# A fused attention and expert kernel: first chunk in two halves, fewer idle products ahead of it, one transfer per expert, one more chunk loaded in both layouts, and a new order table

## The chip, the cores and the metric

The kernel runs on one core of one Trainium2 chip. The metric is the time of one execution on the device, in microseconds (us). Its engines are PE (matrix products, with weight loads shown as PEld), DVE and ACT (which both read PE's results out of PSUM), POOL, and SP, whose queue issues nearly all transfers between HBM and the core's memory.

## The reference

Attention through 32 inducing points, then a mixture of 16 experts, all in float32:

```
B, N, m, C = 4, 10048, 32, 128          # x: (4, 10048, 128), inducing: (32, 128)
def mab(q, kv):                          # softmax attention, kv is key and value
    a = softmax(q @ kv.T / sqrt(C));  return a @ kv
h   = mab(inducing, x)                   # (4, 32, 128): every point looks at all 10048 rows
att = mab(x, h)                          # (4, 10048, 128): every row looks at 32 points
# 4 groups of 4 experts; g = argmax(att @ w_group), e = argmax(att @ w_expert[g])
out = softmax weights of g and e * (relu(att @ w1[g, e]) @ w2[g, e])     # w1 128x1024, w2 1024x128
```

Each row of `att` is a mixture of the 32 rows of `h`. The kernel first takes the case that all rows of a batch pick one expert, applies the expert to the 32 points (one matrix G of 32 rows for each batch) and lets each row mix G. It counts rows for which this does not hold (`n_bad`), and a general branch, not entered here, would redo the work.

## The kernel before, in words

**Tiles.** Each of the 4 batches is cut into 5 chunks (b, k) of 4 x 512 rows (the last of 4 x 480). A chunk comes in transposed from HBM (`xk`, from `xT` or `xL`, 1 MB, C on the partitions). The first attention also needs it untransposed (`xn`). For the chunks in `LOADED` a second transfer brings that layout (`xm`, 1.03 MB); for the others PE turns the chunk (`turn`, four groups of four 128x128 transposes, L139) and ACT or DVE copies each group out (`tev`, in the helper L534).

**First attention** (`att1`, once a chunk): scores `s1` (L152), a running maximum on DVE (`mx`, L156 to L160), exponential on ACT (`ex`, L163), transpose `tr` (L173) with its copy `pev`, product with `xn` (`hq`, L186), accumulation on DVE. **After five chunks** (`mean`, `routes`): `rp`, `ap`, `same`, `hp` (L200 to L230), the routing product `R` (L240, L241), the choice of the expert on DVE (`pick`), then on SP a load of the chosen index (L281) and two transfers, w1 and w2 (L282, L283), into the two halves of one buffer. From these come z (L288), G4 (L306) and G (L312). **Second attention** (`att2`, in groups of two, two and one chunks): scores `s2` (L329), maximum and exponential (L333, L337), logits `L` (L344), gate weights. **Outputs** (`outputs`): 32 products (L383) into four PSUM banks, each emptied in one of three ways: ACT copies it (L398) and POOL scales it by the gate weight (L403); or ACT scales it in four pieces (L396); or DVE scales it (L392). Then SP stores the chunk, 1 MB (L407). 

**What sets the order.** `plan_all` numbers all operations. A table, `ORDER`, lists the numbers in the order of emission, with a letter that chooses the engine; every engine runs its own part of this list strictly in order, SP's transfers included. Buffers are taken from rings (19 large ones, `big`, for chunks, weights and outputs; 8 PSUM banks, `ps`) in the order in which the list frees them. A transfer whose buffer is still in use holds all transfers behind it on SP. Transfers also pass through eight completion semaphores in turn, so that about eight are under way at most.

**Idle products.** `IDLE` names operations ahead of which PE multiplies ones by ones into the bank that the operation is about to take (L489). A size of n stands for n//4 products 512 wide and n%4 products 128 wide. 19 units stand ahead of the first turn of chunk (0, 0); the other eight entries, 29 units, stand after the last R.

## Time and profile before

| | |
|---|---|
| median of 3 runs | 152.69 us (152.15 to 153.06) |
| the profiled execution: its time, its span | 153.44 us, 151.7 us |
| moved by transfers | 56.90 MB, read 35.50 MB, written 20.97 MB |
| busy: PE, DVE, ACT, POOL | 138.2, 112.9, 105.5, 51.1 us |

The span is the stretch that the trace covers. The page cuts it into 40 slices of 3.8 us with a busy share in tenths for each engine; further views give windows of one's choice, the instructions in order of time, the issues of transfers with their time to landing, and the chain of work that ended last. PE counts as busy in nearly all of the span, idle products and stretched waiting products included, so that a full row of PE alone tells little.

### The profile page before, as it was taken

How to read it: one execution, taken by the hardware profiler on the slowest of the kernel's cores; microseconds unless marked ns; L12 is line 12 of the kernel's file. 1: busy time of each engine (PE TensorE's matmuls, PEld its weight loads, DVE VectorE, ACT ScalarE, POOL GpSimd, SP SyncE). 2: the span in 40 equal slices, each digit the busy share in tenths (PEclk: the TensorE clock that was granted, in tenths of full speed). 3: DMA queues.
4: the chain of work that ended last, by engine and by line, in shares of the span. 5: the costliest groups of instructions: out<-in, count | busy, mean ns of one | idle time of the engine just before them, and what ended most of it. 6: DMA issues, size and time to landing. Idle time of an engine off the chain costs nothing.

```text
span 151.7 us, 5598 instructions
## 1 busy us (share of the span) xinstructions
PE 138.2 (91%) x2233; PEld 94.9 (63%) x2233; DVE 112.9 (74%) x383; ACT 105.5 (70%) x265; POOL 51.1 (34%) x70
## 2 busy tenths in 40 slices
PE   6999999999999999999999999999999999999000
PEld 3377588687636777867466786676784666775000
DVE  3056493576689898888998987998989999999500
ACT  3006375477704967788995999989999998999300
POOL 4000000000000000015394702464889998855200
PEclk9999999999999999999999999999999999999955
DMA  4999999999999999999898999979699999999980
GB/s 119 422 426 434 412 425 421 412 431 408 418 404 400 428 417 420 423 418 414 282 337 283 389 411 375 399 294 413 259 406 277 315 417 432 417 417 432 419 352 30
DMA packets 8529, 56.90 MB, mean 375 GB/s; under 512 B 1072, under 2 KB 1072, under 8 KB 2608
## 3 DMA queue, kind: packets, MB, share of 16 engines
q1 hardware_dynamic: 8352, 56.45, 93.1%
q8 instruction: 19, 0.31, 0.8%
q14 instruction: 14, 0.11, 0.2%
q10 hardware_dynamic: 144, 0.03, 0.1%
HBM read 35.50 MB, written 20.97 MB: 372 GB/s over the span
## 4 chain that ended last, share of the span: by engine, by line
PE 67%; DVE 14%; ACT 10%; issue 2%; DVEq 0%; ACTq 0%
PE ps L139 12%; PE ps L152 11%; PE ps L186 9%; PE ps L329 8%; PE ps L383 8%; PE ps L489 5%; PE ps L173 5%; ACT big L398 4%; ACT big L396 3%; PE ps L344 2%; DVE big L392 2%; ACT et L337 1%; DVE mxe L333 1%; PE ps L230 1%; PE ps L306 1%
## 5 line engine op out<-in xcount | busy, mean ns | idle before, releaser
L403 POOL TENSOR_TENSOR big<-big,gate_w 128x512 f32<-128x512 f32 x48 | 48.9, 1050 | 42.8 <-ACT big L398 33.4
L163 ACT ACTIVATE pe<-ps,nb 128x512 f32<-128x512 f32 (+1 forms) x20 | 13.7, 687 | 21.6 <-DVE nb L158 9.9
L398 ACT COPY big<-ps 128x512 f32<-128x512 f32 x48 | 26.7, 625 | 1.7 <-PE ps L383 1.0
L396 ACT ACTIVATE big<-ps,gate_w 128x128 f32<-128x128 f32 x84 | 24.3, 413 | 1.6 <-DVE n_bad L454 1.5
L383 PE MATMUL ps<-G,et 32*128 32x128 f32 x640 | 25.0, 285 | 0.0
L383 PEld LDWEIGHTS ps<-G,et 32*128 32x128 f32 x640 | 21.0, 186 | 5.5 <-ACT big L398 1.9
L139 PE MATMUL ps<-spread,big 128*128 128x128 f32 (+1 forms) x160 | 21.4, 276 | 0.1
L186 PEld LDWEIGHTS ps<-big,pt 128*32 128x32 f32 (+1 forms) x640 | 17.8, 110 | 5.9 <-issue 4.2
L186 PE MATMUL ps<-big,pt 128*32 128x129 f32 (+1 forms) x640 | 21.0, 273 | 0.0
L329 PE MATMUL ps<-big,hT 128*32 128x512 f32 (+2 forms) x192 | 20.5, 525 | 0.0
L152 PE MATMUL ps<-big,small_sb 128*32 128x512 f32 (+1 forms) x160 | 19.9, 588 | 0.0
L139 PEld LDWEIGHTS ps<-spread,big 128*128 128x128 f32 (+1 forms) x160 | 17.8, 141 | 2.9 <-issue 1.0
L156 DVE TENSOR_REDUCE mx<-ps 128x1 f32<-128x512 f32 (+1 forms) x20 | 13.5, 673 | 4.8 <-PE ps L152 4.1
L489 PE MATMUL ps<-ones 128*128 128x128 f32 (+1 forms) x48 | 15.5, 461 | 1.6 <-DVE ones L852 1.5
L129 POOL MEMSET big<- 128x16 f32 x10 | 0.8, 128 | 47.9 <-PE ps L186 44.7
L534 ACT COPY big<-ps 128x512 f32<-128x512 f32 (+1 forms) x28 | 15.6, 592 | 0.8 <-PE ps L139 0.7
L337 ACT ACTIVATE et<-ps,nce 128x512 f32<-128x512 f32 x20 | 13.8, 721 | 2.4 <-DVE nce L334 2.1
L534 DVE COPY big<-ps 128x512 f32<-128x512 f32 x12 | 8.0, 686 | 9.8 <-PE ps L139 9.7
L333 DVE TENSOR_REDUCE mxe<-ps 128x1 f32<-128x512 f32 x20 | 13.3, 667 | 0.7 <-ACT big L398 0.4
L534 ACT COPY pt<-ps 128x512 f32<-128x512 f32 (+2 forms) x20 | 10.0, 523 | 3.5 <-PE ps L173 2.8
L489 PEld LDWEIGHTS ps<-ones 128*128 128x128 f32 x48 | 8.1, 214 | 7.0 <-issue 4.7
L173 PE MATMUL ps<-spread,pe 128*128 128x128 f32 x80 | 12.2, 276 | 0.0
(118 smaller groups left out, 164.6 us busy)
## 6 DMA issues: line engine op xcount, KB each, us to landing
out<-big SPq DMA_DIRECT2D x20, 1024.0 KB, 7.7
big<-xT SPq DMA_DIRECT2D x16, 1024.0 KB, 13.4
big<-xm SPq DMA_DIRECT2D x10, 1032.0 KB, 10.1
big<-w SPq DMA_DIRECT2D x8, 512.0 KB, 6.1
big<-xL SPq DMA_DIRECT2D x4, 960.0 KB, 13.9
small_sb<-small ACTq DMA_DIRECT2D x1, 26.0 KB, 5.9
```

The lines of the kernel that those rows point to most:

```text
L139: em.nc.tensor.transpose(p[:tw, j * P:(j + 1) * P], em.t(xk[b, k])[:, j, off + t * P:off + t * P + tw], em.ident)
L152: em.nc.tensor.matmul(em.t(ps)[32 * j:32 * j + 32, :w], lhsT=em.indT, rhs=em.t(xk[b, k])[:, j, off:], start=True, stop=True)
L173: em.nc.tensor.transpose(p[:tw, t * P:(t + 1) * P], em.t(pe)[:, t * P:t * P + tw], em.ident)
L186: em.nc.tensor.matmul(h[32 * j:32 * j + 32, 0:CS], lhsT=q[:tw, t, 32 * j:32 * j + 32], rhs=x[:tw, t * J + j, :], start=(t == 0), stop=(t = ...
L329: em.nc.tensor.matmul(em.t(ps)[32 * j:32 * j + 32, c0:c1], lhsT=em.hT[b][:, P + 1:P + 1 + M], rhs=em.t(xk[b, k])[:, j, x0:x0 + c1 - c0], s ...
L337: em.nc.scalar.activation(out=em.t(et), in_=em.t(ps), func=AF.Exp, bias=em.s(nc_), scale=1.0)
L383: em.nc.tensor.matmul(em.t(pb[j])[:, t * C:(t + 1) * C], lhsT=em.t(et)[32 * j:32 * j + 32, t * P:(t + 1) * P], rhs=em.Gs[b][32 * j:32 * j ...
L396: em.nc.scalar.activation(out=q[:, t], in_=p[:, t], func=AF.Copy, scale=em.t(gt)["w"][:, r:r + 1])
L398: em.nc.scalar.copy(out=q, in_=p)
L403: em.nc.gpsimd.tensor_tensor(out=q, in0=q, in1=weights(j), op=ALU.mult)
L489: em.nc.tensor.matmul(em.t(ps)[:, 0:w], lhsT=em.ones[:, 0:P], rhs=em.ones[:, 0:w], start=True, stop=True)
L534: (self.nc.scalar.copy if engine == ACT else self.nc.vector.tensor_copy)(out=out, in_=in_)
```

## The change

- The transfer of chunk (0, 0) is cut into two of 0.5 MB (j = 0, 1 and j = 2, 3), with chunk (1, 0) issued between them. Its four turns now each take two column blocks of two j, so that two of them need only the first half; its `s1` is cut in two likewise (`s1j`).
- Ahead of the first turn stand 8 units of idle products, not 19, and 2 more before the first `s1j`. The row of ones is 128 wide and is broadcast to 512 for the wide ones. After the last R stand 37 units, not 29.
- w1 and w2 of an expert lie side by side in a new input, `w12`, and come in one transfer of 1 MB.
- `LOADED` has eleven chunks, not ten: batches 0 and 1 as before; of batches 2 and 3 now (2,0), (2,2), (2,4), (3,0), (3,1), (3,3), (3,4), where it was (2,1), (2,3), (2,4), (3,1), (3,3), (3,4). One chunk less is turned: 36 groups, not 40.
- `ORDER` is a new list of 713 operations (715 before).

```diff
-LOADED = {(0, 2), (0, 4), (1, 1), (1, 3), (2, 1), (2, 3), (2, 4), (3, 1), (3, 3), (3, 4)}
-IDLE = ((2, 19), (455, 3), (465, 2), (515, 3), (625, 4), (635, 2), (657, 4), (667, 5), (704, 6))
+LOADED = {(0, 2), (0, 4), (1, 1), (1, 3), (2, 0), (2, 2), (2, 4), (3, 0), (3, 1), (3, 3), (3, 4)}
+IDLE = ((3, 8), (182, 2), (457, 4), (467, 2), (489, 3), (517, 7), (605, 2), (619, 3), (629, 5), (651, 2), (674, 1), (679, 2), (698, 6))
...
+    def halves(b, k):
+        return [(0, J // 2), (J // 2, J)] if (b, k) == (0, 0) else [(0, J)]
...
-        def fn(e):
-            em.nc.sync.dma_start(out=em.t(xk[b, k]), in_=em.xL[b] if short else em.xT[b, k])
-        xk_at[b, k] = [op("xk", SP, fn, [], [xk[b, k]], size=512 * J * (KL if short else KW))]
+        got = []
+        for j0, j1 in halves(b, k):
+            def fn(e, j0=j0, j1=j1):
+                em.nc.sync.dma_start(out=em.t(xk[b, k])[:, j0:j1], in_=(em.xL[b] if short else em.xT[b, k])[:, j0:j1])
+            got.append(op("xk", SP, fn, [], [] if got else [xk[b, k]], soft=got[-1:], size=512 * (j1 - j0) * (KL if short else KW)))
+        xk_at[b, k] = got
...
-        for t in range(TK):
+        if (b, k) == (0, 0):
+            banks = [(t, t + 2, j, j + 2) for j in (0, 2) for t in (0, 2)]
+        else:
+            banks = [(t, t + 1, 0, J) for t in range(TK)]
...
-            em.nc.sync.dma_start(out=em.t(w12)[:, 0:F], in_=em.w1[bass.ds(i, 1)].rearrange("o d f -> d (o f)"))
-            em.nc.sync.dma_start(out=w2(), in_=em.w2[bass.ds(i, 1)].rearrange("o (p n) d -> p (o n) d", n=FB))
+            em.nc.sync.dma_start(out=em.t(w12), in_=em.w12[bass.ds(i, 1)].rearrange("o p f -> p (o f)"))
...
 ORDER = """
-1a 0a 206a 706a 2a 6a 3b 4a 5b 7b 8a 357a 17a 10a 45a 27a 11a 19a 12a 23a 28a 35a 178a 25a 205a 18a 20a 9a 47a 21a 53a 13a 63a 46a 29a 51a 234a 49a
...
+181a 700a 0a 3a 48a 180a 1a 701a 11a 19a 2a 37a 5a 182a 184a 186a 47a 6a 208a 236a 9a 185b 190a 12a 183a 65a 4b 188a 21a 187a 27a 191a 192a 193a 13a
```

What the new table does is seen at three places. In the rows below, a number behind `ps_` or `big_` is a buffer's; `x4` counts instructions; L numbers of the new kernel are some 10 to 13 higher than the old ones for the same operation.

PE at its start, before. L489 are idle products, L139 turns, L152 `s1`; `big_92` is chunk (0, 0), `big_95` chunk (0, 1).

```order
L489 MATMUL ps_122<-ones 128x512 x4
L489 MATMUL ps_122<-ones 128x128 x3
L139 MATMUL ps_122<-spread,big_92 128x128 x4
L139 MATMUL ps_123<-spread,big_92 128x128 x4
L139 MATMUL ps_124<-spread,big_92 128x128 x4
L139 MATMUL ps_125<-spread,big_92 128x128 x4
L152 MATMUL ps_126<-big_92,small_sb 32x512 x4
L152 MATMUL ps_127<-big_95,small_sb 32x512 x4
```

And after. L501 are idle products, L149 turns, L165 `s1`; `big_92` is again chunk (0, 0), `big_94` is chunk (1, 0).

```order
L501 MATMUL ps_122<-ones 128x512 x2
L149 MATMUL ps_122<-spread,big_92 128x128 x4
L501 MATMUL ps_123<-ones 128x128 x2
L165 MATMUL ps_124<-big_92,small_sb 32x512 x2
L149 MATMUL ps_125<-spread,big_92 128x128 x4
L149 MATMUL ps_123<-spread,big_94 128x128 x4
L149 MATMUL ps_126<-spread,big_94 128x128 x4
L149 MATMUL ps_127<-spread,big_94 128x128 x4
L149 MATMUL ps_128<-spread,big_92 128x128 x4
L165 MATMUL ps_129<-big_94,small_sb 32x512 x4
L165 MATMUL ps_124<-big_92,small_sb 32x512 x2
```

PE now begins on a half chunk; chunk (1, 0) fills the time until the second half of (0, 0).

SP at its start, before: all loads of `xT` or `xL`; after the first come (0, 1), (0, 3), (0, 2), (1, 0), (1, 2) and (0, 4).

```order
L116 DMA big_92<-xT 128x2048
L116 DMA big_95<-xT 128x2048
L116 DMA big_96<-xT 128x2048
L116 DMA big_97<-xT 128x2048
L116 DMA big_98<-xT 128x2048
L116 DMA big_99<-xT 128x2048
L116 DMA big_101<-xL 128x1920
```

And after: half of (0, 0), (1, 0), the other half, (0, 1), (0, 2), (0, 3), (0, 4).

```order
L121 DMA big_92<-xT 128x1024
L121 DMA big_94<-xT 128x2048
L121 DMA big_92<-xT 128x1024
L121 DMA big_95<-xT 128x2048
L121 DMA big_97<-xT 128x2048
L121 DMA big_98<-xT 128x2048
L121 DMA big_101<-xL 128x1920
```

Only one chunk of batch 1 now stands ahead of the end of batch 0, where two stood.

SP from the third expert's weights to the last expert's, before. L121 is a load of an untransposed chunk, L407 a store, L281 the read of the chosen index.

```order
L282 DMA big_105<-w 128x1024
L283 ISA
L283 DMA big_105<-w 128x1024
L121 DMA big_109<-xm 128x2064
L407 DMA out<-big_108 128x2048
L407 DMA out<-big_98 128x2048
L407 DMA out<-big_97 128x2048
L407 DMA out<-big_91 128x2048
L407 DMA out<-big_93 128x2048
L281 TENSOR_LOAD pi_1821
```

And after, where L419 is a store and L294 the read of the index:

```order
L295 DMA big_101<-w 128x2048
L419 DMA out<-big_99 128x2048
L419 DMA out<-big_98 128x2048
L419 DMA out<-big_100 128x2048
L419 DMA out<-big_107 128x2048
L419 DMA out<-big_102 128x2048
L294 TENSOR_LOAD pi_1832
```

The last load of a chunk now stands ahead of the third expert's weights. In both lists four stores stand ahead of the third expert's weights, five between them and the last expert's, and eleven behind those.

## The prediction

> **What bounds the kernel now.** I read the page first, then the start in order of time, the transfers' landings, a table of windows, and the chain of waits.

> ```profile
> span 151.7 us, 5598 instructions
> DVE  3056493576689898888998987998989999999500
> ACT  3006375477704967788995999989999998999300
> DMA  4999999999999999999898999979699999999980
> PE 67%; DVE 14%; ACT 10%; issue 2%; DVEq 0%; ACTq 0%
> ```

> ACT and DVE are half empty in the first third and full in the last, while the transfer engines are full nearly throughout. The windows tell the stages apart (columns: PE, PEld, DVE, ACT, POOL busy with instruction counts, clock, transfer share, GB/s):

> ```profile
> 3.00:6.50 3.50, 3.50 (x5) 1.35 (x4) 0.00 (x0) 0.00 (x0) 0.00 (x0) 1.00 1.00 410
> 8.60:60.00 51.40, 51.15 (x756) 36.43 (x758) 37.38 (x109) 30.04 (x63) 0.26 (x2) 1.00 1.01 418
> 60.00:95.00 35.00, 35.00 (x645) 24.26 (x635) 30.43 (x115) 29.57 (x74) 13.37 (x14) 1.00 0.97 371
> 95.00:121.00 26.00, 25.81 (x514) 17.67 (x505) 23.63 (x87) 24.94 (x69) 19.55 (x20) 1.00 0.90 337
> 121.00:143.00 22.00, 19.09 (x329) 13.16 (x329) 20.06 (x69) 19.50 (x59) 16.07 (x16) 1.00 1.01 423
> ```

> Against the 423 GB/s of the last stage, the queue loses (423-371) x 35 + (423-337) x 26 = 4.06 MB of carrying between 60 and 121 us, worth 9.6 us. Before 60 and after 121 it loses next to nothing. ACT has 5.4 us idle from 60 to 95 and 1.1 us from 95 to 121. The end itself is the queue's:

> ```profile
> 113.46 1.06 SPq L283 DMA_DIRECT2D big<-w  x1
> big<-w SPq DMA_DIRECT2D x1, 512.0 KB, 7.1
> 114.62 28.60 SPq L407 DMA_DIRECT2D out<-big  x11
> 142.89 0.33 SPq L407 DMA_DIRECT2D out<-big  x1
> out<-big SPq DMA_DIRECT2D x1, 1024.0 KB, 7.6
> ```

> The last expert's weights land at 113.46 + 7.1 = 120.6. Behind them go eleven stores, 11 x 1.049 MB / 423 GB/s = 27.3 us, so the last could land at 147.9; it lands at 142.89 + 7.6 = 150.5, 1.2 us ahead of the end. So the time is when the last expert's weights are through the queue, plus about 30 us. These weights wait for the last R, and what leads there is PE until 96 us and then ACT, as the chain of waits has it (start, length, what):

> ```profile
> 94.35 0.88 PE ps L186 x32
> 95.23 1.10 PE ps L383 x29
> 96.39 0.59 ACT big L398
> ...
> 105.91 0.41 ACT hs L217
> ```

> **The start.** Rows in order of time, with the landings:

> ```profile
> 0.75 0.39 SPq L116 DMA_DIRECT2D big<-xT  x1
> big<-xT SPq DMA_DIRECT2D x1, 1024.0 KB, 5.8
> 1.46 7.29 PE L489 MATMUL ps<-ones 128*128 128x512 f32 x14 [1.46 <-DVE ones L852]
> 5.89 0.34 PEld L489 LDWEIGHTS ps<-ones 128*128 128x128 f32 x1 [0.52 <-issue]
> 6.75 0.34 PEld L489 LDWEIGHTS ps<-ones 128*128 128x128 f32 x1 [0.52 <-issue]
> 7.49 0.19 PEld L489 LDWEIGHTS ps<-ones 128*128 128x128 f32 x1 [0.41 <-issue]
> 7.92 0.64 PEld L489 LDWEIGHTS ps<-ones 128*128 128x128 f32 x5 [0.24 <-issue]
> 8.59 1.91 PE L139 MATMUL ps<-spread,big 128*128 128x128 f32 x16
> 10.43 1.92 PE L152 MATMUL ps<-big,small_sb 128*32 128x512 f32 x16
> ```

> Chunk (0, 0) has landed at 0.75 + 5.8 = 6.55, and PE multiplies ones until 8.59: 2.04 us given away. The first half, 0.524 MB less at 410 GB/s, should land 1.28 us earlier, at 5.3. The new idle products, two wide ones of two passes at 0.86 us (5.89 to 6.75), run from about 1.2 to 4.6, so PE waits some 0.7 us, then works. But PE cannot keep all of it, since the queue delivers at its own pace:

> ```profile
> 4.19 0.44 SPq L116 DMA_DIRECT2D big<-xL  x1
> big<-xL SPq DMA_DIRECT2D x1, 960.0 KB, 18.2
> 9.01 0.33 SPq L116 DMA_DIRECT2D big<-xT  x1
> big<-xT SPq DMA_DIRECT2D x1, 1024.0 KB, 20.8
> 26.02 0.96 PE L152 MATMUL ps<-big,small_sb 128*32 128x464 f32 x8
> 32.38 1.09 PE L139 MATMUL ps<-spread,big 128*128 128x128 f32 x8
> ```

> The chunk issued at 4.19 lands at 22.4 and is first used at 26.02; the one issued at 9.01 lands at 29.8 and is used at 32.38. So a load lies 2.6 to 3.6 us before its use, and 2.0 us at the first. PE can run ahead by 2 to 2.6 us until it meets the queue. Bounds: -2.3 us, and +0.3 where the clock (below) takes it back. I take -1.7, nearer the full gain, since work runs in a stretch in which PE had none.

> **The turn that goes.** Sixteen transposes took 8.59 to 10.43, so four groups cost 1.84 us, which PE no longer spends. PE is on the path until 96 us, so all of it counts: -1.84 (bound 0, where ACT holds the same place). Its four evictions lie beside PE and count as nothing; were that cover gone, they would be worth 4 x 0.59 = 2.4 us of ACT:

> ```profile
> L534 ACT COPY big<-ps 128x512 f32<-128x512 f32 x27 | 15.1, 592 | 0.8 <-PE ps L139 0.7
> L534 DVE COPY big<-ps 128x512 f32<-128x512 f32 x12 | 8.0, 686 | 9.8 <-PE ps L139 9.7
> L398 ACT COPY big<-ps 128x512 f32<-128x512 f32 x48 | 26.7, 625 | 1.7 <-PE ps L383 1.0 <-issue 0.7
> L396 ACT ACTIVATE big<-ps,gate_w 128x128 f32<-128x128 f32 x84 | 24.3, 413 | 1.6 <-DVE n_bad L454 1.5
> L489 PE MATMUL ps<-ones 128*128 128x128 f32 x32 | 5.0, 283 | 0.1
> ```

> **What the table does to ACT.** Over the whole list ACT copies 52 banks instead of 48 (26.7 / 48 = 0.556 us each) and scales 19 in four pieces instead of 21 (4 x 24.3 / 84 = 1.16 us each), with two more `tev`: +2.2 - 2.3 + 1.1 = +1.0 us. DVE loses two scalings and six `tev` at about 8.0 / 12 = 0.67 us: -5 us. Behind the third expert's load the list holds 30 copies in both, but 12 four-piece scalings instead of 14: 2.3 us of ACT work moved forward, out of the stage that ACT fills and into the one where it has 5.4 us idle. This is what lets the earlier PE through to the last R; by itself I count it 0 (bounds -2.3 and +1.0). POOL's 4 more scalings end nothing.

> **The loads and the queue.** One more `xm`, 1.057 MB / 423 GB/s = 2.5 us. It is issued ahead of the third expert's weights, where the queue loses 9.6 us anyway, and that is its cover; without it, it costs all 2.5. It can still make a store behind it late, so of 0 to 2.5 I take +1.0. On SP, (1, 0) is moved ahead of the second half of (0, 0); this delays the end of that chunk to about 5.3 + 2.5 + 1.3 = 9.1, while PE holds one turn of (0, 0) and three of (1, 0) for that time. One transfer fewer for each expert saves SP one issue (1.06 us in the row of L283), but the bytes are the same and the queue behind is never empty there, so I take 0 (bound -1.1). It also spares a semaphore of the eight, which the halves use once.

> **Idle products in the tail.** 8 units more, at most 0.31 us each (5.0 / 32 a record, two records a unit): 2.5 us on a PE whose other work is then below its time. I take 0; the bound is +1, if they hold a bank that another product wants.

> **Sum.** -1.7 - 1.84 + 1.0 = -2.5 us. The profiled execution took 153.44 us (span 151.7 and 1.7 around it) and would take 150.9; the median of the runs lies 0.75 lower, so I say 152.69 - 2.5 = 150.2 us. The eleven stores at the end are as before.

> **Rivals.**
> *The clock stays low.* Up to 6.75 the passes stand 0.86 us apart, then 0.74, then 0.43: PE ran at half pace until about 7.4, 5.9 us after its first product. If it needs 5.9 unbroken us, and the new start breaks at 4.6, full pace comes at 5.3 + 5.9 = 11.2, by which PE has done 2.95 us of work; before it had done 2.6. The gain is then 0.3 and the time 151.6. If the waits for (1, 0) near 7.8 break it again, full pace comes at 13.7 with some 3.9 us done against 5.1: 1.2 us behind, 153.0. I take 152.3. Against it: the order holds idle products and `s1j` in the gap. [...]

> ```profile
> 21.53 2.35 PE L139 MATMUL ps<-spread,big 128*128 128x128 f32 x20
> ```

> After the start PE does nothing but transposes for over 2 us and their pace (0.11 us each) does not fall, though that shows a clock kept, not one gained.

> *The queue is the bound (slower).* If the 9.6 us of gaps come from buffers and from SP's strict order, not from late outputs, the earlier PE fills none of them, and the load adds 2.5 us: 155.2. It decides once the gaps shrink by less than 2.5 us. For it: the transfers are at 418 to 423 GB/s outside those stages. Against it: the eleven stores took 2.6 us more than the queue needs, so outputs are late, and those move with PE and ACT.

> *ACT sets the end and nothing changes.* ACT has 1.0 us more work and was busy 24.94 of 26 us from 95 to 121. If it cannot start earlier, PE's 3.5 us end as waiting: 152.7.

> *More is gained.* If the load hides wholly and the start gives its 2.3: -4.1, and a little from ACT's forward 2.3, 148.2.

> **How the numbers follow.** Chances: forecast 0.52 (149.0 to 151.5), clock 0.15, queue 0.12, ACT 0.13, more 0.08. The range 148.2 to 152.9 leaves out the queue case and about a third of the clock's. A change of 0.5% (0.76 us) is about what can be told from none. Faster: 0.51 of the forecast, all of "more", a third of the clock's and 0.02 of ACT's, 0.66. Slower: the queue and a third of the clock's, 0.17. Same: the rest, 0.17, most of it ACT's.

> **What would show it.** Right: the first turn at about 5.3; the pace of products doubling by 7.5 to 8; the first R about 2 us earlier; the last expert's weights landing near 118 with the queue at 380 GB/s or more from 60 to 121; eleven stores behind them as before. Wrong: half pace beyond 11 us, chunk loads landing after PE is ready for them, or 371 and 337 GB/s again in the middle.

## The result, and the profile after

| | before | after |
|---|---|---|
| first comparison, 4 runs each | 152.42 us (151.93 to 153.06) | 154.3 us (153.87 to 154.92) |
| second comparison, 23 and 12 runs | 152.91 us (152.00 to 153.39) | 154.73 us (151.45 to 157.58) |
| profiled execution of the first comparison: time, span | 153.44, 151.7 us | 154.92, 153.1 us |

The forecast was 150.2 us, 2.5 us less than before; the first comparison shows 1.88 us more. The ratio of the first comparison is 1.0107 with an interval of 1.0063 to 1.0150. The second gives 0.9970 (0.9928 to 1.0012), but such a ratio leaves out every run more than 1.5% above the fastest of its kernel, and here the scatter itself is the result; so from here on the text goes by medians of all runs, less the median of the kernel before in the same comparison: +1.88 and +1.82 us. The scatter is the kernel's own, since three kernels of the table below (e7, e13, e19) scatter by 0.5 us or less.

The page of the kernel after: its span, three rows of 40 slices, and the chain by engine.

```profile
span 153.1 us, 5560 instructions
DVE  3006285264799997889959988988889988999700
ACT  3024847835646778994989979857879889899500
DMA  3999999999999999999899999999999999999970
PE 75%; DMA 9%; DVE 7%; issue 2%; ACT 1%; SPq 0%; DVEq 0%; ACTq 0%
```

The chain has moved from ACT (10%, now 1%) to PE and to transfers (9%). The same windows as before say where:

```profile
8.60:60.00 51.40, 51.35 (x729) 35.31 (x726) 33.15 (x105) 32.59 (x71) 0.25 (x2) 1.00 1.01 420
60.00:95.00 35.00, 35.00 (x673) 25.63 (x677) 29.74 (x110) 30.24 (x79) 14.54 (x15) 1.00 0.98 383
95.00:121.00 26.00, 24.86 (x461) 15.83 (x457) 22.65 (x83) 20.63 (x53) 21.09 (x21) 1.00 0.98 364
121.00:143.00 22.00, 20.90 (x377) 15.19 (x369) 19.67 (x67) 19.90 (x58) 16.76 (x17) 1.00 0.99 411
```

From 95 to 121 us ACT is busy 20.63 us, not 24.94: the relief came. By the prediction's own measure the queue now loses (423-383) x 35 + (423-364) x 26 = 2.93 MB, worth 6.9 us in place of 9.6. The gaps shrank by 2.7 us, about the 2.5 us that the added load needs, and no more: from 60 to 121 us the queue carried 1.1 MB more than before, and the load has 1.06 MB. But PE, which hardly idled from 95 to 121 us before (busy 25.81 of 26), now idles 1.1 us there. The view of waits names what it waits for, of before and then of after (total, times, longest):

```profile
PE ps L489 <- DVE ones L852: 1.5, 1, 1.5
PE ps L451 <- DVE t L447: 0.5, 1, 0.5
```

```profile
PE ps L395 <- issue: 1.3, 3, 0.9
PE ps L501 <- DVE ones L864: 1.1, 1, 1.1
PE ps L149 <- DMA big<-xT: 1.0, 1, 1.0
PE ps L300 <- DMA big<-w: 0.8, 1, 0.8
```

The new waits are of three kinds: one at the start for the first half chunk (L149), one for the last expert's weights (L300), and three, 1.3 us together, with no releaser at all ("issue") in the middle of the output products L395. Two of these last three and the one for the weights lie on the chain of waits:

```profile
99.24 0.25 issue
...
105.14 0.89 issue
...
113.81 8.82 DMA big<-w
```

The start in order of time (PE alone):

```profile
1.06 3.78 PE L501 MATMUL ps<-ones 128*128 128x512 f32 x4 [1.06 <-DVE ones L864]
...
5.81 1.09 PE L149 MATMUL ps<-spread,big 128*128 128x128 f32 x4 [0.97 <-DMA big<-xT]
...
7.68 1.92 PE L165 MATMUL ps<-big,small_sb 128*32 128x512 f32 x4
```

The first turn begins at 5.81 instead of 8.59, but PE is at half pace until 9.68 us (7.37 before), and half a `s1` (L165) takes 1.92 us, as long as two whole ones did in the row of before (10.43). R of the first batch starts at 39.54 us against 39.98: of 2.8 us, 0.44 are left, and the later waits take more than that.

### The profile page after: what moved, and what is told of

It reads as the page before. It is cut to its first block, busy times and chain, and to the rows that moved or that the text cites. A ratio compares the mean times of both kernels' runs of the same rounds, so it can differ in the third digit from the quotient of the medians.

```text
span 153.1 us, 5560 instructions
## 1 busy us (share of the span) xinstructions
PE 138.7 (91%) x2227; PEld 95.0 (62%) x2227; DVE 108.5 (71%) x375; ACT 106.3 (69%) x263; POOL 55.5 (36%) x73
## 4 chain that ended last, share of the span: by engine, by line
PE 75%; DMA 9%; DVE 7%; issue 2%; ACT 1%; SPq 0%; DVEq 0%; ACTq 0%
PE ps L165 13%; PE ps L199 12%; PE ps L149 11%; PE ps L395 11%; PE ps L341 8%; PE ps L186 6%; DMA big<-w 6%; DMA big<-xT 3%; PE ps L501 3%; PE ps L356 3%; PE ps L300 1%; DVE big L404 1%; PE ps L318 1%; PE ps L234 1%; PE ps L243 1%
## 5 line engine op out<-in xcount | busy, mean ns | idle before, releaser
L415 POOL TENSOR_TENSOR big<-big,gate_w 128x512 f32<-128x512 f32 x52 | 53.3, 1049 | 49.2 <-ACT big L410 46.0
L410 ACT COPY big<-ps 128x512 f32<-128x512 f32 x52 | 28.4, 597 | 6.8 <-PE ps L395 4.6
L395 PE MATMUL ps<-G,et 32*128 32x128 f32 x640 | 25.0, 284 | 1.3 <-issue 1.3
L546 ACT COPY big<-ps 128x512 f32<-128x512 f32 (+1 forms) x30 | 16.9, 595 | 12.2 <-PE ps L149 12.1
L395 PEld LDWEIGHTS ps<-G,et 32*128 32x128 f32 x640 | 20.8, 186 | 6.9 <-issue 3.5
L165 PE MATMUL ps<-big,small_sb 128*32 128x512 f32 (+1 forms) x160 | 22.7, 601 | 0.0
L408 ACT ACTIVATE big<-ps,gate_w 128x128 f32<-128x128 f32 x76 | 22.1, 391 | 0.8 <-PE ps L395 0.3
L149 PE MATMUL ps<-spread,big 128*128 128x128 f32 (+1 forms) x144 | 19.6, 280 | 1.0 <-DMA big<-xT 1.0
L149 PEld LDWEIGHTS ps<-spread,big 128*128 128x128 f32 (+1 forms) x144 | 16.3, 143 | 6.0 <-issue 5.2
L501 PE MATMUL ps<-ones 128*128 128x128 f32 (+1 forms) x58 | 15.4, 399 | 1.1 <-DVE ones L864 1.1
L186 PE MATMUL ps<-spread,pe 128*128 128x128 f32 x80 | 12.2, 278 | 0.0
L501 PEld LDWEIGHTS ps<-ones 128*128 128x128 f32 x58 | 9.0, 209 | 5.1 <-issue 2.9
L186 PEld LDWEIGHTS ps<-spread,pe 128*128 128x128 f32 x80 | 8.9, 140 | 2.4 <-ACT big L546 0.8
## 6 DMA issues: line engine op xcount, KB each, us to landing
out<-big SPq DMA_DIRECT2D x20, 1024.0 KB, 6.8
big<-xT SPq DMA_DIRECT2D x15, 1024.0 KB, 13.5
big<-xm SPq DMA_DIRECT2D x11, 1032.0 KB, 13.7
big<-w SPq DMA_DIRECT2D x4, 1024.0 KB, 8.0
big<-xT SPq DMA_DIRECT2D x2, 512.0 KB, 6.5
```

The costliest lines, as they stand in the source:

```text
L149: em.nc.tensor.transpose(p[:tw, n * P:(n + 1) * P], em.t(xk[b, k])[:, j, off + t * P:off + t * P + tw], em.ident)
L165: em.nc.tensor.matmul(em.t(ps)[32 * j:32 * j + 32, :w], lhsT=em.indT, rhs=em.t(xk[b, k])[:, j, off:], start=True, stop=True)
L186: em.nc.tensor.transpose(p[:tw, t * P:(t + 1) * P], em.t(pe)[:, t * P:t * P + tw], em.ident)
L395: em.nc.tensor.matmul(em.t(pb[j])[:, t * C:(t + 1) * C], lhsT=em.t(et)[32 * j:32 * j + 32, t * P:(t + 1) * P], rhs=em.Gs[b][32 * j:32 * j ...
L408: em.nc.scalar.activation(out=q[:, t], in_=p[:, t], func=AF.Copy, scale=em.t(gt)["w"][:, r:r + 1])
L410: em.nc.scalar.copy(out=q, in_=p)
```

## The experiments

Besides the kernel before, eighteen kernels ran. `R` is the start of the first batch's routing product R, "full" the time from which the trace grants the full clock, both of the profiled execution. The runs stand in several comparisons, each with the kernel before beside it; the last column, "less before", is the median less that of the kernel before in the same comparison.

| kernel | median us (range) | full | R | less before |
|---|---|---|---|---|
| before | 152.91 (152.00 to 153.39) | 7.37 | 39.98 | 0 |
| after, second comparison | 154.73 (151.45 to 157.58) | 4.65 | 38.55 | +1.82 |
| e1 weights in two | 153.97 (152.46 to 156.95) | 5.02 | 38.81 | +1.01 |
| e2 before, joint weights | 151.99 (151.40 to 153.26) | 5.15 | 38.89 | -0.97 |
| e3 s1 whole | 152.98 (151.28 to 156.62) | 9.47 | 38.65 | +0.02 |
| e4 19 idle products | 154.99 (154.60 to 156.17) | 6.68 | 39.97 | +2.03 |
| e5 e1 and e3 | 153.78 (151.69 to 157.25) | 10.29 | 38.89 | +0.87 |
| e7 old table, new start, joint weights | 150.99 (150.78 to 151.17) | 6.86 | 37.93 | -1.92 |
| e8 one load twice | 160.75 (160.17 to 161.62) | 4.79 | 38.81 | +7.84 |
| e10 e7 with eleven chunks | 152.85 (152.36 to 153.36) | 5.45 | 37.99 | +0.06 |
| e11 code shifted by 112 | 153.91 (151.77 to 154.98) | 5.11 | 38.03 | +1.12 |
| e12 code shifted by 176 | 155.85 (152.55 to 158.39) | 10.23 | 39.86 | +3.06 |
| e13 e7 with s1 in halves | 151.09 (150.92 to 151.42) | 6.66 | 38.35 | -1.70 |
| e14 after, first chunk first | 152.03 (151.26 to 154.59) | 4.02 | 37.48 | -0.42 |
| e15 after, ten chunks | 157.68 (156.53 to 158.43) | 9.14 | 39.30 | +5.23 |
| e16 e14 with ten chunks | 156.25 (155.80 to 156.88) | 7.03 | 37.71 | +3.80 |
| e17 after, 10 idle products | 152.70 (151.58 to 158.08) | 6.48 | 38.62 | +0.15 |
| e18 e14, 10 idle products | 152.70 (150.90 to 154.69) | 5.88 | 37.41 | +0.15 |
| e19 e7, weights in two | 151.34 (151.18 to 151.43) | 6.12 | 37.95 | -1.21 |

The first theory after comparing the two profiles was the joint transfer: z of the last expert reads only w1, which landed at 119.26 before, and now waits until 122.64 for both matrices. Its rivals were the queue's bytes and the start.

**e1 and e2: the joint transfer, undone in the new kernel and alone in the old one.**

```diff
-            em.nc.sync.dma_start(out=em.t(w12), in_=em.w12[bass.ds(i, 1)].rearrange("o p f -> p (o f)"))
+            em.nc.sync.dma_start(out=em.t(w12)[:, 0:F], in_=em.w1[bass.ds(i, 1)].rearrange("o d f -> d (o f)"))
+            em.nc.sync.dma_start(out=w2(), in_=em.w2[bass.ds(i, 1)].rearrange("o (p n) d -> p (o n) d", n=FB))
```

> The changed kernel with w1 and w2 of each expert as two transfers of 512 KB again; all else as in the changed kernel. Joint theory: in the changed kernel the first layer z of the last expert waits at 122.77 us for the end of the one transfer of 1024 KB (issued 113.81), though it reads the first half alone; as two transfers the first lands some 1.3 to 2.8 us earlier (before: w1 119.26, w2 120.60), z starts at about 120 to 121.5 and the end comes 1.3 to 2.5 us earlier: 151.8 to 153.0 us. Queue theory: the bytes are the same and the DMA queue is full until 121 us, so the stores end where they ended: within 0.5 us of the changed kernel's 154.3, even if z starts earlier. Start theory: nothing here touches the first 13 us, so it too gives 153.8 to 154.8.

> The kernel before with only this part of the change: w1 and w2 of each expert in one transfer of 1024 KB. Joint theory: z of the last expert, at 119.96 us behind w1 in the kernel before, waits for the whole, which lands near 120.6 (where w2 landed) to 122: 0.6 to 2 us later, and the end as much: 153.0 to 154.4 us. Queue theory: same bytes, so the last store, which was limited by the queue in the kernel before (issued 142.89, landed 150.46), lands where it did: 151.9 to 152.9. By the prediction's step (nothing, bound -1.1) 151.3 to 152.4.

In e2 the joint transfer is a gain of 0.97 us (ratio 0.9953, 0.9923 to 0.9984). z does wait for the whole (0.8 us at 119.85), but that whole lands at 119.71, when before only w1 had landed at 119.26 and w2 at 120.60. e1 lies 0.8 us under the second comparison of the change, within a scatter of 4.5 us. The joint theory falls as an explanation of the loss.

**e3 and e4: the start.** e3 emits the four products of the first `s1` in one place; e4 sets 19 idle products.

```diff
-                for j in range(j0, j1):
+                for j in (range(j0, j1) if j1 - j0 == J else range(J) if j0 else ()):
```

```diff
-IDLE = ((3, 8), (182, 2), ...
+IDLE = ((3, 19), (182, 2), ...
```

> The changed kernel with the four products s1 of the first chunk in one place (where the second half stood) and none at the place of the first half; turns and transfers still in halves. Halved-products theory: the first half took 1.85 us at the low clock (7.68 to 9.53), the second 0.96 at 12.81, while four products in four column groups take 0.86, so the first batch's table R (39.54 us) comes 1 to 1.9 us earlier; the end moves by as much only where no transfer ends the wait later: 152.4 to 154.3. Joint or queue theory: later stages wait for transfers (z of the last expert at 122.77 for its weights), so the early gain is lost: 153.8 to 154.8. For the clock: if the half products (not transposes) are what kept TensorE counted as busy, full pace comes later than the 9.7 us of the changed kernel; if idle time alone is what counts, not later than 9.7.

> The changed kernel with 19 idle products ahead of the first chunk in place of 8, as in the kernel before. Clock theory: full pace comes near 7.4 us as in the kernel before and not at 9.7; the first turns wait until the idle products end (about 7.4 us and not 5.8), then the turns and the first s1 half run at 0.43 in place of 0.85 per pass, so R of the first batch comes within 0.5 us of the changed kernel's 39.54, earlier or later. The end: 153.6 to 154.8 by the joint and the queue theory; by a theory that lays the loss on the low clock at the start alone it would come back to some 152.5.

e3's median lies 1.8 us under the change's, within a scatter of 5.3 us: R came 0.9 us earlier than in the change's first profile although full pace came as late (9.47). In e4 full pace came at 6.68 and R at 39.97, as forecast, but the turns waited for the idle products, and the time was 154.99. So the low clock alone isn't the loss; in the profiles so far an R near 39.5 to 40, for whatever reason, goes with 154 to 155 us in this table (39.54 with 154.92, 39.97 with 154.60). The old table's profiled run took 153.44 from 39.98.

**e9: the change once more, beside the others.** No edit.

> The changed kernel once more, unchanged, on the chip of the runs beside it, since its four first runs stood against four of the kernel before, and since full pace of TensorE came at 9.68 us in its profile but at 5.02 us in the profile of the kernel with split weights, which has the same instructions up to 13 us. If the loss is real it is 1.005 to 1.015 again: 153.8 to 155.0 us. If the late clock of that one profile made it, the time is nearer to 152.5 to 153.5.

The median of +1.82 us is the loss of the first comparison again, but its runs lie anywhere from 151.45 to 157.58. The profiled one took 152.50 us, and so the same program can be read in two executions 2.5 us of span apart. Its start and its waits:

```profile
5.87 0.63 PE L149 MATMUL ps<-spread,big 128*128 128x128 f32 x4 [1.06 <-DMA big<-xT]
...
6.88 1.05 PE L165 MATMUL ps<-big,small_sb 128*32 128x512 f32 x4
```

```profile
PE ps L149 <- DMA big<-xT: 1.1, 1, 1.1
PE ps L501 <- DVE ones L864: 1.1, 1, 1.1
PE ps L300 <- ACT et L349: 0.4, 1, 0.4
PE ps L165 <- DMA big<-xL: 0.4, 1, 0.4
PE ps L395 <- issue: 0.3, 1, 0.3
```

Full pace came at 4.65, ahead of the hole for the first half, and R at 38.55, 0.99 us earlier than in the first profile. Product by product, this lead stays 0.99 us until 60 us, is 1.29 at 79, 1.64 at 99.5, 2.75 at 106 and 2.88 at z of the last expert. Its two largest steps, 0.35 and 1.11 us, are at the waits without releaser; the first profile has three of them, this one a single one of 0.3 us.

**e5: both s1 whole and the weights in two**, the edits of e1 and e3 together.

> The changed kernel with both parts undone that gained by themselves: s1 of the first chunk whole (0.9943 of the kernel before) and w1, w2 in two transfers (1.0002). If the two are independent (0.9 us of TensorE at the start, and the wait of the last expert's z) they add up: about 0.984 to 0.990, 150.5 to 151.5 us. If both only make room for the same wait (z of the last expert for its weights), they don't: 0.993 to 1.000, 152 to 153 us.

They don't add: +0.87, between e3 alone and e1 alone. Whatever they change is lost in the scatter. The profile fell on the slowest run (157.25 us) although R came at 38.89: it has two waits without releaser, of 1.12 us (to 79.51) and 1.57 us (to 107.32), and behind the second the clock is half from 109.28 to 112.69.

**e7: the old table and ten chunks with the new start.** The table, `LOADED` and the later idle products are those of before, renumbered; the halves, both issued first, 8 idle products, `s1` whole, joint weights.

```diff
-IDLE = ((2, 19), (455, 3), ...
+IDLE = ((3, 8), (456, 3), ...
-1a 0a 206a 706a 2a 6a 3b 4a 5b 7b 8a ...
+2a 0a 1a 207a 707a 3a 5a 4b 7a 8b 6b 9a ...
```

> The table, the ten untransposed chunks and the idle products of the kernel before, with the start of the change (first chunk in two halves, both issued ahead of the second chunk, 8 idle products in place of 19, s1 whole) and the joint transfer of an expert. If the new table with its eleventh chunk is what costs, this is faster than the kernel before with the joint transfer alone (0.9953, idle products until 7.65 us): by the turns' earlier start, 0.5 to 1.5 us, so 150.4 to 151.5 us. If the queue of that table is bound behind the start, it is the same as that one: 151.7 to 152.4 us.

150.99 us, six runs within 0.4 us, ratio 0.9864 (0.9844 to 0.9885): the fastest of all, 0.95 us under e2. So the start and the joint transfer do gain; the loss is in the rest of the change.

**e8: the queue made fuller.**

```diff
-                em.nc.sync.dma_start(out=em.t(xn[b, k]), in_=em.xm[b, k])
+                for _ in range(2 if (b, k) == (3, 1) else 1):
+                    em.nc.sync.dma_start(out=em.t(xn[b, k]), in_=em.xm[b, k])
```

> The changed kernel with the load of one untransposed chunk (batch 3, chunk 1; 1.06 MB; landed near 88 us) issued twice in a row into the same buffer, so the queue carries 1.06 MB more, 2.5 us at its 420 GB/s. Queue theory: everything behind it in the queue lands 2.5 us later, the last weights and the last store too: 156.2 to 157.0 us. TensorE theory (the table ends by TensorE's work, and the queue has slack between 88 and 105 us): 154.0 to 155.2 us.

Both theories fell short: 2.5 us of transfer cost 6.0. PE now waits for chunks, and one row of slices shows the rest (granted clock in tenths):

```profile
PE ps L166 <- DMA big<-xL: 2.3, 2, 1.8
PE ps L200 <- DMA big<-xm: 2.1, 1, 2.1
```

```profile
PEclk9999999999999999999999996599999999999955
```

PE waits 2.06 us (to 95.59) and 1.77 us (to 98.44); within the second wait the clock falls, and it is half from 96.95 to 103.77 us. So these waits are paid twice.

**e10: an eleventh chunk in the old table.** e7 with (3, 0) loaded untransposed behind its first load; its four turns and evictions fall away.

```diff
-LOADED = {..., (2, 4), (3, 1), (3, 3), (3, 4)}
+LOADED = {..., (2, 4), (3, 0), (3, 1), (3, 3), (3, 4)}
```

> The kernel with the old table and the new start (old idle products but 8 at the start, s1 whole, joint weights; 0.9864 of the kernel before) with an eleventh untransposed chunk: batch 3, chunk 0 is loaded a second time untransposed (1.06 MB) right behind its first load, and its 16 turns and 4 evictions fall away; nothing else moves. Queue theory: 2.5 us more in the queue against 1.75 us less of TensorE, and the code of TensorE is fetched later: 0.5 to 3 us slower than that kernel, 151.5 to 154 us. If the new table and not the bytes cost the time: the same or up to 1.8 us faster, 149.2 to 151.2.

+1.98 us against e7. PE has less to do (134.8 us busy, 136.2 in e7) and waits more. None of these four lines is in e7's view (a choice of the lines):

```profile
PE ps L197 <- DMA big<-xm: 0.8, 1, 0.8
PE ps L163 <- DMA big<-xT: 0.7, 2, 0.5
PE ps L393 <- ACT G L544: 0.5, 1, 0.5
PE ps L197 <- issue: 0.4, 1, 0.4
```

The load stands in another place than in the change. In e10 it is one of three issued at 44.64 to 48.13 us, in the stretch before 60 us where the queue is full, and what stands behind it lands 2.5 us later than in e7 (the second expert's weights at 79.33, not 76.83). The change issues it at 68.31 us, in the stretch with gaps. So e10 prices a load in a full queue, and not the cover that the prediction counted on.

**e11 and e12: the waits without releaser.** The rows of L395, of before (L383) and after, show them as idle time:

```profile
L383 PE MATMUL ps<-G,et 32*128 32x128 f32 x640 | 25.0, 285 | 0.0
```

```profile
L395 PE MATMUL ps<-G,et 32*128 32x128 f32 x640 | 25.0, 284 | 1.3 <-issue 1.3
q8 instruction: 19, 0.31, 0.8%
```

They stand where neither an operand nor a bank is missing. Counted from the first, weight loads and the queue's own instructions included, PE resumes at its instructions 3009, 3265 and 4033: distances of 256 and 3 x 256. In e4, with ten products' instructions more ahead, the wait of 0.75 us stands at 3265 again, another place of the program. And the trace has 19 packets of 16,384 bytes on the queue "instruction". In the profile after, the three landed 1.29, 1.35 and 1.33 us ahead of the instruction that had waited; in all profiles such a wait ends 1.1 to 1.6 us behind a packet, and in the kernel before no packet lands less than 1.67 us ahead of its block. By these distances and packets PE's code comes in blocks of 256 instructions, and these came late. In the profiles before and after each of the first sixteen packets falls into a block of its own, 0.2 to 4.9 us after that block has begun. Over all profiles the packets start up to 5.1 us after the block ahead of theirs has begun (6.3 once in e8) and take about 1 us, so a block that PE runs through in 5.4 us can be too short. Sixteen such waits stand in the profiles, every one at a multiple of 256 instructions from these, give or take two, all in kernels with eleven untransposed chunks (11 of 13); the seven kernels with ten, of either table, have none. The two kernels shift where blocks end, by splitting the products s1 of the first seven or eleven chunks:

```diff
+                for c0, c1 in ((0, w // 2), (w // 2, w)) if b * NK + k < SPLIT else ((0, w),):
-                    ... em.t(ps)[32 * j:32 * j + 32, :w], rhs=...[:, j, off:]
+                    ... em.t(ps)[32 * j:32 * j + 32, c0:c1], rhs=...[:, j, off + c0:off + c1]
```

> The changed kernel with the products s1 of the first seven chunks as two of 256 columns each: the same columns, 112 more instructions on TensorE ahead of 31 us, so that the blocks of 256 instructions in which its code comes end 112 instructions earlier in the program. In the fast profile of the changed kernel the shortest block between 70 and 135 us takes 5.4 us (98 to 103 us); with ends 112 instructions earlier it would be 6.0. Code theory (a block is asked for when the one ahead begins, waits 3 to 5 us for the full DMA engines, takes 0.95 and is usable 1.35 us later, so a block shorter than 5.3 to 7.3 us makes TensorE wait): fewer waits and less scatter, most runs between 152 and 154 plus what the splitting costs at the start (to be read from R of the first batch, 0 to 1 us). Queue or weights theory: scatter as in the changed kernel, 151.5 to 157.6, median 154.7 or more.

> The same with the first eleven chunks' s1 in two: 176 more instructions ahead of about 45 us. In the fast profile of the changed kernel the shortest block would then take 4.5 us, near 85 us, where the wait for a packet was 2.6 to 4.2 us. Code theory: TensorE waits some 0.5 to 1.5 us at that place in nearly every run, and the time is worse than with seven split: 154.5 to 157. Queue or weights theory: the same as with seven split but for the splitting itself (0 to 0.6 us).

With 112, PE's view of waits has none without releaser, and this is the shortest profile of the new table as the change starts it (150.0 us); but the median is +1.12 and the runs still reach 154.98. With 176 one came at 81.30 us, near the foreseen place, of 0.54 us, and a late weight besides:

```profile
PE ps L302 <- DMA big<-w: 1.9, 1, 1.9
PE ps L503 <- DVE ones L866: 1.1, 1, 1.1
PE ps L150 <- DMA big<-xT: 0.9, 1, 0.9
PE ps L503 <- DVE big L406: 0.6, 1, 0.6
PE ps L167 <- issue: 0.5, 1, 0.5
```

Late code is thus a part of the loss and not all of it: between the two profiles of the change it is 1.46 of the 2.88 us. How much of the medians it makes, six runs each of e11 and e12 do not tell.

**e13: the halves of s1 in the steady kernel.** e7 with two products behind the first two turns and two behind the others.

```diff
-        got = [op("s1", PE, mm, xk_at[b, k], [ps])]
+            got.append(op("s1" if j1 - j0 == J else "s1j", PE, mm, [at], [] if got else [ps], soft=got[:1]))
```

> The kernel with the old table and the new start, with s1 of the first chunk in halves as in the change (two products behind the turns of the first half, two behind those of the second). Halved-products theory: each half takes what the whole took, so R of the first batch comes 0.9 us later at full clock, up to 1.9 at the low one, and this table hands a start on to its end: 151.7 to 152.7 us (that kernel: 150.99). If the halves hide behind the wait for the second half: 150.8 to 151.3.

R comes 0.42 us later, the median is 0.1 higher (0.22 in the column "less before"): the halves cost little when the clock is up. In the second profile of the change a half takes 1.05 us at full clock (its row at 6.88), and a whole one in e3 takes 1.07; so two halves cost as much as two whole ones.

**e14 to e16: start or bytes.** e14 keeps the change but issues both halves, their turns and s1 ahead of all else; e15 keeps the change's start and takes the eleventh chunk's second load out of the new table, turns put back; e16 does both.

```diff
-181a 700a 0a 3a 48a 180a 1a 701a 11a 19a 2a 37a 5a 182a ...
+181a 700a 0a 1a 2a 3a 180a 48a 701a 5a 4b 7a 6a 9a 8b 11a 10a 12a 19a 37a 182a ...
```

```diff
-LOADED = {..., (2, 4), (3, 0), (3, 1), (3, 3), (3, 4)}
+LOADED = {..., (2, 4), (3, 1), (3, 3), (3, 4)}
```

> The changed kernel (new table, eleven untransposed chunks, joint weights) with another order of the first chunk alone: both halves issued ahead of every other load, their turns and both halves of s1 ahead of those of the second chunk, as in the kernel with the old table and the new start. Sensitivity theory (the new table hands a late start on to its end two to three times over: R of the first batch at 38.55 us went with an end at 152.5, at 39.54 with 154.9, at 39.97 with 154.6): R comes at 37.9 to 38.4 us in most runs and the time is 151.0 to 152.5 with little scatter. Queue theory (eleven chunks fill the queue whatever the start): scatter and median as in the changed kernel, 153.5 to 155.

> The changed kernel with ten untransposed chunks: the second, untransposed load of batch 3, chunk 0 is taken out and its 16 turns (4 banks) and 4 evictions are put back, two on each of ACT and DVE, between places of the new table that are otherwise untouched. Queue theory: 2.5 us less in the queue, the code of TensorE is fetched sooner, the weights land sooner: median 151.5 to 153, less scatter than 151.5 to 157.6. Table theory (the order, and not the bytes, loses): the 1.75 us of turns come on top, 155.5 to 157.

> Both together: the new table with the first chunk's loads and turns first, and ten untransposed chunks. Queue theory: as with ten chunks, and the start's 0.5 to 1 us come through: 150.8 to 152. Sensitivity theory: as with the start alone, and the turns put back cost their 1.75 us: 152.5 to 154.

e14's median lies 2.2 us under the change's with all bytes kept. e15 and e16 lose 3.4 and 4.2 us against the change and e14, more than the 1.75 of the turns, and the weights land later, not sooner (126.15 in e15):

```profile
PE ps L300 <- DMA big<-w: 1.5, 1, 1.5
```

So fewer bytes don't mend this table in this form: with the turns put back the third and the last expert's weights are issued at 100.17 and 116.68, against 95.99 and 113.81 in the change. Where the turns were put back was chosen by hand, so e15 doesn't measure the share of the bytes.

**e17 to e19: the hole.** In the nine profiles with a hole of 0.87 to 1.06 us ahead of the first half, full pace came at 4.65, 4.79, 5.02, 5.11 or at 9.14, 9.47, 9.68, 10.23, 10.29; with a smaller one or none (eleven profiles) always between 4.02 and 7.37.

```diff
-IDLE = ((3, 8), (182, 2), ...
+IDLE = ((3, 10), (182, 2), ...
```

> The changed kernel with 10 idle products ahead of the first chunk in place of 8: two more of 128 columns, which fill the hole of 0.9 to 1.06 us between the last idle product (4.84 us at the low clock) and the landing of the first half (5.7 to 5.8). In the nine profiles with that hole full pace came either by 5.11 us or not before 9.14; in the six without it between 4.02 and 7.37. Hole theory: full pace by 7.5 us, R of the first batch by 39.0 us, and with it fewer of the late runs: median 152.3 to 153.7. Rival (the hole has nothing to do with the clock, or a start of 39.0 is late enough for the later waits): median 154 to 155, up to 157.5.

> The same two idle products added to the changed kernel with the first chunk's loads and turns first (152.03 us, 151.26 to 154.59), where the hole is 0.2 to 0.7 us. Hole theory: the two late runs of twelve go, 151.2 to 152.4. Rival: the same scatter, 151.3 to 154.6, median 152 to 152.5.

> The fastest kernel so far (old table, new start, ten chunks, joint weights; 150.99 us) with w1 and w2 as two transfers, so that only the joint transfer is undone. By the joint transfer's own gain on the kernel before (0.9953): 151.5 to 152.0 us. If z of the last expert, which waits 0.55 us for the whole there, gains from its half alone: 150.3 to 150.9.

e17 is the smallest edit of all: two idle products of 128 columns, and the median falls from 154.73 to 152.70 (by 1.67 us in the column "less before"), with 11 of 12 runs between 151.58 and 153.81. The size is uncertain, as the change's own runs scatter by 6 us; the count of late runs tells more. Of the sixteen runs of the change in both comparisons, nine lie more than 1.5 us above the median of the kernel before; of the twelve each of e14, e17 and e18 it is two, one and two. The hole is gone:

```profile
1.06 4.64 PE L501 MATMUL ps<-ones 128*128 128x512 f32 x8 [1.06 <-DVE ones L864]
5.72 0.99 PE L149 MATMUL ps<-spread,big 128*128 128x128 f32 x4
...
7.09 1.05 PE L165 MATMUL ps<-big,small_sb 128*32 128x512 f32 x4
```

e18 didn't gain over e14. Its profile fell on a late run, with full pace at 5.88 and R early, at 37.41, and shows another part of the scatter, the code of block 3265 late and the clock halved behind it:

```profile
104.34 0.50 PE L395 MATMUL ps<-G,et 32*128 32x128 f32 x8 [1.77 <-issue]
```

e19: the joint transfer is worth 0.35 us on e7 by the plain medians, 0.71 us in the column "less before".

## Why the prediction was wrong, step by step

- **What bounds the kernel.** Held. The last weights landed at 122.64 us and the last store 28.7 us later; 119.75 and 29.6 in the second profile of the change, 118.50 and 29.9 in e7. The forecast of 118 for the weights was 4.6 us off, a little more than the profiled execution's error (150.9 forecast, 154.92 measured).
- **The start, -1.7.** The step that failed is "PE waits some 0.7 us, then works". The first half landed at 5.67 us, not 5.3, and the turn began at 5.81 behind a hole of 0.97 us. With such a hole full pace came in five of nine profiles 1.8 to 2.9 us later than in any without it, and in four as early as without. Two executions of one program got the one and the other (9.68 and 4.65 us for the change; see the last section). R of the first batch came 0.44 us earlier in the first profile and 1.43 in the second. With the hole filled the median was 1.67 us lower (e17), a size that the scatter leaves uncertain. With both halves first and the old table the start gave 0.95 us (e7 against e2): right in kind, too large by 0.75.
- **The rival "the clock stays low".** It named this mechanism, with a break at 4.6, and laid full pace at 11.2 for 151.6 or, broken once more, at 13.7 for 153.0; it came at 9.68. Its price was wrong, since a microsecond at the start was taken to be a microsecond at the end. In the new table R went from 38.55 to 39.54 and the end of the span from 150.6 to 153.1. In all twenty profiles full pace came at 10.29 us at the latest, so neither 11.2 nor 13.7 was reached.
- **The turn that goes, -1.84, and the loads and the queue, +1.0.** Together -0.84. The step that failed is "PE is on the path until 96 us, so all of it counts". The table cuts the span of six profiles in four, at the start of the first and the last batch's R and at the landing of the last weights (us):

| | before | after | second profile | e14 | e7 | e10 |
|---|---|---|---|---|---|---|
| start to first R | 39.98 | 39.54 | 38.55 | 37.48 | 37.93 | 37.99 |
| first R to last R | 69.42 | 70.62 | 69.06 | 69.00 | 69.40 | 70.58 |
| last R to landing of the last weights | 11.20 | 12.48 | 12.14 | 12.07 | 11.17 | 11.22 |
| that landing to the end | 31.06 | 30.51 | 30.89 | 31.51 | 30.79 | 30.95 |

Between the first and the last R the second profile of the change and e14 gain 0.36 and 0.42 us, not 1.84; the first profile loses 1.20, of which 1.14 are its two waits for code there. Then the way from the last R to the landing, where the prediction put no loss, grows by 0.87 to 1.28 us, so that nothing of PE's gain is left. By medians the new table with the eleventh chunk costs +1.50 us (e14 against e7, where `s1` is in halves as well). The cover, "where the queue loses 9.6 us anyway", is not shown to have failed: the gaps took up the 1.1 MB. e10 (+1.98 against e7) is no test of it, as its load stands in the full stretch; there it costs 1.18 us between the first and the last R.

- **What the table does to ACT, 0.** The relief was there (24.94 to 20.63 us); what it was worth was not measured by itself.
- **One transfer for each expert, 0 with a bound of -1.1.** Measured -0.97 and -0.71 in the old table, near the bound: the term was mis-sized.
- **Idle products in the tail, 0.** Not tried by themselves.
- **The rivals "the queue is the bound", 155.2, and "ACT sets the end", 152.7.** The first one's figure is nearest to the median, and its rule (gaps shrink by less than 2.5 us) met a measured 2.7, so it stood at its threshold. But it held that PE's earliness is worthless, and e7 shows the contrary (0.95 us under e2 by the start alone); e14 and e17 point the same way. Against the second, ACT's share of the chain fell from 10% to 1%.

As steps from one kernel to the next, each with the scatter of its two medians: -0.97 (joint) -0.95 (start) +1.50 (table and eleventh chunk, halves of s1) +0.57 (e18 against e14) 0.0 (e17 against e18: chunk (1, 0) between the halves) +1.67 (the hole, second comparison against e17) make +1.82 us. The steps are differences of neighbours, so they must add up; the last three are within the scatter.

What stays open: why the code packets came later in the profile with the later start (4.25 us behind the start of the block ahead in the first profile of the change, 3.14 in the second, for the same block); which part of the +1.50 is the table's and which the eleventh chunk's; and why the last weights take longer behind the last R.

e7 beats both kernels: 0.9864 of the kernel before.

## What to carry to other kernels

Before a median is believed, look at the scatter: here two executions of one program differ by 2.5 us of span, and their profiles side by side name the waits that did it. When a start is moved forward, fill the hole that it leaves ahead of the first data; here two idle products went with a median 1.7 us lower and with one late run in twelve in place of nine in sixteen. In e10 a load put into a full stretch of the queue made what stood behind it land 2.5 us later. And time saved on PE counts only as far as the waits behind it pass it on (here 0.36 and 0.42 of 1.84 us from the first R to the last).

## What the runs showed of the hardware that was not expected

```profile
5.84 1.08 PE L149 MATMUL ps<-spread,big 128*128 128x128 f32 x4 [0.99 <-DMA big<-xT]
6.72 1.06 PE L501 MATMUL ps<-ones 128*128 128x128 f32 x4
7.57 3.29 PE L149 MATMUL ps<-spread,big 128*128 128x128 f32 x20
10.78 1.07 PE L165 MATMUL ps<-big,small_sb 128*32 128x512 f32 x8
```

Of the step of 3.413 us that ended at 9.47, only some 0.9 us (6.72 to 7.57) were other products than turns.
